# Transposing w_sg by DMA instead of on TensorE in a fused attention and gMLP kernel, with its step list ordered anew

## Chip, cores, metric

One core of one Trainium2 chip. The metric is the device time of one execution in microseconds (us). A run is called slow when it is more than 1.5% above the fastest run of the same kernel; in the rounds of the experiments the fast runs of the kernel before lie between 158.9 and 160.9 us. Ratios and verdicts use fast runs only; medians are over all runs.

## The reference

Windowed attention with four sink tokens, followed by a gMLP block. For each of 4 batches (8 heads, 768 positions, head size 64):

```python
scores = q @ k.T / sqrt(64)                # kept: the first 4 keys, and the last 128
x   = softmax(scores) @ v                  # heads side by side: 768 x 512
h   = gelu(x @ w_in)                       # 512 -> 1024; u = h[:, :512], v = h[:, 512:]
v_n = (v - mean) / sqrt(var + 1e-6) * g_ln
v_s = w_sg @ v_n + b_sg                    # w_sg is 768 x 768, over positions
out = x + (u * v_s) @ w_out
```

The kernel computes in bf16 with f32 accumulation. The spatial product needs `w_sg` with its rows turned into columns; `w_sg` is loaded once, turned once, and used by all four batches.

## The kernel before

The whole kernel is one list of steps. Every engine takes the instructions of its steps in the order of the list, so the list is the schedule. Nearly all loads are issued by GpSimd, also in list order, and stand among its other work. `mm_ring` is a ring of four PSUM buffers, `sc_ring` one of two: a step that takes a buffer waits until its last reader is done. In both kernels q and k of batch 3, and x of batches 2 and 3, are turned by DMA already.

| step | what it does | engine |
|---|---|---|
| `LQ LK LV LW LWS LWO` | loads of q, k, v, w_in, w_sg (two halves), w_out | GpSimd issues |
| `TQ`, `TK`; `EQ`, `EK` | turn four or two heads of q or k; copy from PSUM | TensorE; VectorE (`.D`) or ScalarE (`.A`) |
| `QK`, `EX`, `MK`, `SX` | scores, exponentials, masks, exponentials of the sinks | TensorE, ScalarE, VectorE or GpSimd, ScalarE |
| `AV`, `NR`, `XT`, `XE` | weighted values, normalisation, turn of x, its copy | TensorE, VectorE, TensorE, VectorE or ScalarE |
| `MA`/`MV`, `UA`/`MU`; `GV`, `GU` | w_in products, v half and u half; gelu | TensorE; ScalarE |
| `BN RS NM Z` | layer norm | VectorE, GpSimd, VectorE, both |
| `WT`; `WE` | turn a row block of w_sg; bring it into `wsgT` | TensorE; VectorE, or DMA |
| `SP`, `GT`, `GM` | spatial product, its bias, the gate | TensorE, VectorE, VectorE or GpSimd |
| `OU OB`, `RA RB`, `ST SB` | w_out product, addition of x, store | TensorE, VectorE, SyncE |

The first number of a step is the batch. The parts that matter here:

```python
def WT(ti):                                    # six turns on TensorE into one PSUM buffer
    fresh(mm_ring, ("w", ti))
    ps = psb(("w", ti))
    for si in range(NT):
        nc.tensor.transpose(ps[:, si, :], wsg_rows[:, ti, 128 * si:128 * (si + 1)], iden)

def WE(ti):
    if ("w", ti) not in mm_ring.held:          # no WT before it: one DMA transpose on SyncE
        return nc.sync.dma_start_transpose(out=wsgT[:, :, 128 * ti:128 * (ti + 1)], in_=wsg_rows[:, ti, :])
    nc.vector.tensor_copy(wsgT[:, :, 128 * ti:128 * (ti + 1)], psb(("w", ti)))

def SP(b, hf, dc):
    ps = fresh(mm_ring, ("g", b, hf, dc))
    for si in range(NT):
        nc.tensor.matmul(ps[:, 0:NH], z[b][:, si, 128 * dc:128 * (dc + 1)],
                         wsgT[:, si, NH * hf:NH * (hf + 1)], start=(si == 0), stop=(si == NT - 1))
# ... cut ...
for step in STEPS.split():
    name, *idx = step.split(".")
    done[step] = code[name](*(int(i) if i.isdigit() else i for i in idx))
```

The softmax here doesn't subtract the row's maximum and nothing guards it: scores larger than these inputs give would overflow.

Of the kernel before, what the change touches and what calls it, by code (L numbers as in the profile page):

```python
# [13 lines left out]


STEPS = """
ZERO IDEN LQ.0.0 LK.0.0 LQ.0.1 FILL LK.0.1 LC MASK VSK LK.0.2 MASK0 CQ.0.0.D LK.0.3 HM.7 TQ.0.0 CK.0.0.D LQ.0.2
EQ.0.0.A TK.0.0 LQ.0.3 EK.0.0.A TQ.0.1 LV.0.0 KS.0.0 QK.0.0.2 EQ.0.1.D QK.0.0.0 SK.0.0 EX.0.0.2 LV.0.1 VSM.0 TK.0.1
LV.0.2 EK.0.1.D HM.1 TK.0.2 EX.0.0.0 QK.0.0.1 LQ.1.0 MK.0.0.2.D KS.0.1 TK.0.3 EK.0.2.A LV.0.3 MK.0.0.0 QK.0.1.2 SK.0.1
EX.0.0.1 EK.0.3.D LW.0 SX.0.1 KS.0.2 QK.0.1.1 KS.0.3 LW.1 EX.0.1.2 MK.0.0.1.D TQ.0.2 TQ.0.3 EX.0.1.1 EQ.0.2.D QK.0.1.0  # L20
LWS.0 AV.0.0.1 EX.0.1.0 EQ.0.3.D QK.0.2.0 MK.0.1.1.P SK.0.2 EX.0.2.0 NR.0.0.1 AV.0.0.0 QK.0.3.1 LWS.1 NR.0.0.0 SK.0.3
EX.0.3.1 QK.0.3.0 MK.0.1.0 LQ.1.2 EX.0.3.0 QK.0.2.1 MK.0.1.2.D LK.1.0 AV.0.1.0 MK.0.2.0 AV.0.1.1 EX.0.2.1 MK.0.3.1.P
NR.0.1.0 QK.0.3.2 SX.0.3 QK.0.2.2 NR.0.1.1 EX.0.3.2 LK.1.2 TQ.1.0 MK.0.2.1.D XT.0.2 EX.0.2.2 LWO TQ.1.1 MK.0.3.0
EQ.1.0.A AV.0.2.0 XE.0.2.D MK.0.3.2.P EQ.1.1.A NR.0.2.0 AV.0.3.0 XT.0.0 MK.0.2.2.P NR.0.3.0 AV.0.3.1 XE.0.0.D LQ.2.0
XT.0.1 AV.0.2.1 NR.0.3.1 MA.0.0 XE.0.1.D NR.0.2.1 MV.0.0 VSM.1 LV.1.0 XT.0.3 GV.0.0 VSM.3 UA.0.0 VSM.2 MU.0.0 LG WT.1
LV.1.1 XE.0.3.A BN.0.0 WT.2 WT.0 GU.0.0 MV.0.2 WE.2 WE.1 MV.0.1 WE.0 LV.1.2 GV.0.2 BN.0.2 MU.0.3 GV.0.1 WT.3 BN.0.1
RS.0.2 GU.0.3 WT.5 TQ.1.3 LV.1.3 TQ.1.2 EQ.1.3.A MU.0.1 WE.5 RS.0.1 EQ.1.2.A WE.3 NM.0.2 MU.0.2 GU.0.1 LQ.2.2 Z.0.4.D
NM.0.1 Z.0.5.A Z.0.1.D TK.1.0 Z.0.3.D GU.0.2 TK.1.1 LV.2.0 Z.0.2.D TK.1.2 EK.1.0.A Z.0.0.D TK.1.3 EK.1.1.D EK.1.2.A
QK.1.0.2 QK.1.0.0 SP.0.0.2 EK.1.3.A EX.1.0.0 LV.2.1 KS.1.0 WT.4 SP.0.0.0 GT.0.0.2 WE.4 SK.1.0 GT.0.0.0 SP.0.1.2
EX.1.0.2 LV.2.2 MK.1.0.0 SX.1.0 GM.0.0.0.D QK.1.1.2 GT.0.1.2 QK.1.0.1 LK.2.0 TQ.2.0 EX.1.1.2 GM.0.0.2.D TQ.2.1  # L30
GM.0.1.2.D EX.1.0.1 SP.0.1.0 MK.1.1.2.D LK.2.2 MK.1.0.2.D EQ.2.1.A QK.1.1.0 MK.1.0.1.D QK.1.1.1 EQ.2.0.A SP.0.1.1
LV.2.3 GT.0.1.0 EX.1.1.1 AV.1.0.0 GM.0.1.0.P GT.0.1.1 AV.1.0.1 EX.1.1.0 NR.1.0.0 SP.0.0.3 GM.0.1.1.P NR.1.0.1 QK.1.2.2
LV.3.0 GT.0.0.3 QK.1.3.0 EX.1.2.2 SP.0.0.1 MK.1.1.1.D LV.3.1 EX.1.3.0 MK.1.1.0 TQ.2.2 AV.1.1.1 GT.0.0.1 MK.1.2.2.P
EQ.2.2.A QK.1.2.1 NR.1.1.1 QK.1.2.0 LV.3.2 EX.1.2.1 TQ.2.3 GM.0.0.1.D AV.1.1.0 GM.0.0.3.D EX.1.2.0 XT.1.2 LV.3.3
MK.1.3.0 OU.0.0 NR.1.1.0 EQ.2.3.A MK.1.2.1.P QK.1.3.1 XE.1.2.D QK.1.3.2 EX.1.3.1 XT.1.0 RA.0.0 OU.0.1 MK.1.2.0
EX.1.3.2 ST.0.0 LK.3.0 TK.2.0 XE.1.0.D AV.1.2.0 RA.0.1 EK.2.0.A AV.1.2.1 NR.1.2.0 ST.0.1 TK.2.1 MK.1.3.1.P TK.2.3
NR.1.2.1 EK.2.1.A TK.2.2 QK.2.0.0 EK.2.3.A EK.2.2.D MK.1.3.2.P QK.2.0.2 AV.1.3.0 EX.2.0.0 SP.0.1.3 NR.1.3.0 LK.3.2
EX.2.0.2 KS.2.0 AV.1.3.1 QK.2.1.2 GT.0.1.3 QK.2.1.1 EX.2.1.2 SK.2.0 NR.1.3.1 XT.1.1 MK.2.0.2.P EX.2.1.1 OU.0.2
XE.1.1.D GM.0.1.3.P SX.2.0 QK.2.1.0 RA.0.2 QK.2.0.1 EX.2.1.0 XT.1.3 LQ.3.0 MK.2.1.1.D OU.0.3 ST.0.2 XE.1.3.A
MK.2.1.2.D MV.1.0 MK.2.0.0 EX.2.0.1 RA.0.3 LQ.3.2 MK.2.0.1.D ST.0.3 MV.1.1 GV.1.0 MK.2.1.0 AV.2.1.0 OU.0.4 GV.1.1  # L40
BN.1.0 MV.1.2 EK.3.1 RA.0.4 MU.1.0 BN.1.1 GV.1.2 AV.2.0.1 ST.0.4 EK.3.2 GU.1.0 MU.1.3 BN.1.2 RS.1.1 OU.0.5 GU.1.3
NM.1.1 RS.1.2 MU.1.1 Z.1.3.A EK.3.3 RA.0.5 Z.1.0.A Z.1.1.D NM.1.2 MU.1.2 Z.1.2.A NR.2.1.0 Z.1.4.D GU.1.1 AV.2.0.0
Z.1.5.D EQ.3.0 GU.1.2 AV.2.1.1 NR.2.0.1 QK.2.2.0 NR.2.0.0 QK.2.2.2 SP.1.1.0 EX.2.2.0 NR.2.1.1 SP.1.0.0 ST.0.5 EQ.3.1
GT.1.1.0 GM.1.1.0.P SP.1.0.3 EX.2.2.2 GT.1.0.0 MK.2.2.0 QK.2.3.0 EQ.3.3 QK.2.2.1 GT.1.0.3 GM.1.0.0.P EX.2.3.0 SP.1.0.2
MK.2.2.2.D EX.2.2.1 SP.1.1.2 GM.1.0.3.D MK.2.3.0 EQ.3.2 QK.2.3.1 GT.1.1.2 MK.2.2.1.P QK.2.3.2 SP.1.1.1 EX.2.3.1
GT.1.0.2 GM.1.1.2.D EX.2.3.2 AV.2.2.0 MK.2.3.1.P EK.3.0 GT.1.1.1 SP.1.0.1 NR.2.2.0 GM.1.0.2.P AV.2.3.0 GT.1.0.1
QK.3.1.1 MK.2.3.2.P QK.3.1.2 NR.2.3.0 AV.2.2.1 EX.3.1.1 SP.1.1.3 XD.2.0 GM.1.0.1.P NR.2.2.1 EX.3.1.2 AV.2.3.1
MK.3.1.1.P GT.1.1.3 QK.3.0.1 NR.2.3.1 QK.3.0.0 MK.3.1.2.P EX.3.0.1 OU.1.1 EX.3.0.0 KS.3.0 OU.1.0 MK.3.0.1.P RA.1.1
XD.2.1 SK.3.0 RA.1.0 QK.3.0.2 SX.3.0 QK.3.1.0 OU.1.2 MK.3.0.0 EX.3.0.2 GM.1.1.1.D EX.3.1.0 AV.3.0.0 GM.1.1.3.D MV.2.0
MK.3.0.2.P RA.1.2 MK.3.1.0 ST.1.1 ST.1.0 ST.1.2 OU.1.3 GV.2.0 OU.1.4 MV.2.1 BN.2.0 MV.2.2 GV.2.1 RA.1.4 RA.1.3 ST.1.4  # L50
OU.1.5 GV.2.2 BN.2.1 ST.1.3 MU.2.2 BN.2.2 MU.2.0 RS.2.1 GU.2.2 MU.2.3 GU.2.0 NM.2.1 RS.2.2 RA.1.5 Z.2.3.A Z.2.0.D
ST.1.5 MU.2.1 Z.2.1.A NM.2.2 NR.3.0.0 GU.2.3 Z.2.5.D AV.3.1.0 Z.2.4.D GU.2.1 AV.3.0.1 NR.3.1.0 QK.3.3.1 QK.3.2.0
AV.3.1.1 EX.3.3.1 Z.2.2.D NR.3.0.1 SP.2.1.2 NR.3.1.1 SP.2.0.3 GT.2.1.2 EX.3.2.0 MK.3.3.1.P QK.3.3.0 GT.2.0.3 SP.2.1.3
EX.3.3.0 GM.2.1.2.D GM.2.0.3.D QK.3.2.1 MK.3.2.0 QK.3.3.2 SP.2.0.2 EX.3.2.1 MK.3.3.0 GT.2.1.3 EX.3.3.2 AV.3.3.0
MK.3.2.1.P GT.2.0.2 SP.2.0.1 NR.3.3.0 MK.3.3.2.P AV.3.2.0 GT.2.0.1 QK.3.2.2 SP.2.0.0 GM.2.0.2.P NR.3.2.0 EX.3.2.2
GM.2.1.3.D XD.3.0 AV.3.3.1 MK.3.2.2.P GT.2.0.0 SP.2.1.0 NR.3.3.1 GM.2.0.0.P AV.3.2.1 GT.2.1.0 SP.2.1.1 GM.2.0.1.D
NR.3.2.1 GM.2.1.0.P OU.2.0 GT.2.1.1 XD.3.1 OU.2.1 GM.2.1.1.D RA.2.0 OU.2.5 RA.2.1 MU.3.0 RA.2.5 MV.3.0 GU.3.0 ST.2.5
ST.2.0 ST.2.1 OU.2.2 GV.3.0 MV.3.1 BN.3.0 MV.3.2 GV.3.1 RA.2.2 BN.3.1 ST.2.2 MU.3.1 GV.3.2 OU.2.3 BN.3.2 RS.3.1 GU.3.1
MU.3.3 NM.3.1 RS.3.2 RA.2.3 Z.3.3.A MU.3.2 Z.3.2.D ST.2.3 Z.3.1.A NM.3.2 Z.3.0.D OU.2.4 Z.3.5.A Z.3.4.D GU.3.2
SP.3.0.1 RA.2.4 GU.3.3 ST.2.4 SP.3.0.2 GT.3.0.1 GM.3.0.1.P SP.3.0.3 GT.3.0.2 GM.3.0.2.D SP.3.0.0 GT.3.0.3 GM.3.0.3.P  # L60
SP.3.1.0 GT.3.0.0 GM.3.0.0.P SP.3.1.3 GT.3.1.0 GM.3.1.0.P OU.3.1 GT.3.1.3 SP.3.1.1 GM.3.1.3.P RA.3.1 ST.3.1 OU.3.0
GT.3.1.1 SP.3.1.2 GM.3.1.1.P RA.3.0 ST.3.0 OU.3.2 GT.3.1.2 GM.3.1.2.P RA.3.2 ST.3.2 OU.3.5 OU.3.3 RA.3.5 ST.3.5 OB.3.5
RA.3.3 OU.3.4 RB.3.5 ST.3.3 SB.3.5 RA.3.4 ST.3.4
"""


# [5 lines left out]
TURN = ('SSSS', 'SSSS', 'SSSS', 'DDDD')  # L72


LAST = (5,)


@with_exitstack
def kernel(
# [477 lines left out]
    def cols_of(b, t, second=False):  # L557
        n = d_model // 2 if b == B - 1 and t in LAST else d_model
        return slice(n, 2 * n) if second else slice(0, n)
# [74 lines left out]
```

## Time and profile before

| | us |
|---|---|
| two runs before the prediction | 161.38 and 159.85, median 160.62 |
| the profiled run of them (slow state) | 162.22 |
| the same kernel in the rounds of the experiments, medians | 159.25 to 159.71 |

The profiled run was in the slow state, and that mattered. Its page shows a lower granted clock in two early slices (third and fourth digit) and these transfers. The clock digits are tenths of full speed in 40 slices of the span, and q1 is the queue of the transfers that SyncE issues:

```profile
PEclk9968999999999999999999999999999999999998
...
DMA packets 63154, 22.70 MB, mean 141 GB/s; under 512 B 51360, under 2 KB 60064, under 8 KB 63136
...
q1 hardware_dynamic: 17648, 10.66, 25.6%
```

TensorE's stretches as the slow profile has them stand in the prediction below. There the first w_in product of batch 0 starts at 28.3 us and TensorE has hardly a gap after it (0.3 us up to 150 us). In the traced fast run of the old order (e3 below) that product starts at 24.4 us, and TensorE then comes to loads that have not landed, as the experiments show.

### The profile page before, as it was taken

What the parts mean: (1) busy time and instruction counts of PE and PEld (TensorE: products, weight loads), DVE (VectorE), ACT (ScalarE), POOL (GpSimd) and SP (SyncE); (2) the same over time, 40 slices, a digit from 0 to 9 for tenths busy, and PEclk for the clock granted to TensorE, in tenths of its full rate; (3) what the DMA queues carried; (4) which work ended last, traced back from release to release, by engine and by line L of the source; (5) the groups of instructions that cost most, each with busy time, mean ns of one, the idle gap of its engine ahead of it and who ended that gap; (6) DMA issues with size and microseconds to landing.
All of it is one profiled execution on the core that took longest, in us unless ns stands there. A gap on an engine that the chain in (4) does not pass through costs nothing.

```text
span 160.5 us, 3811 instructions
## 1 busy us (share of the span) xinstructions
PE 147.8 (92%) x1520; PEld 86.9 (54%) x1520; DVE 130.2 (81%) x303; ACT 99.9 (62%) x117; POOL 86.4 (54%) x118
## 2 busy tenths in 40 slices
PE   4588867999999999999999999999999999999980
PEld 1245456657656667655665673445756644555530
DVE  4459999979998999897798889689889945976661
ACT  3168995438999797995697747835986225480000
POOL 7996898226854999990405595204038600216620
PEclk9968999999999999999999999999999999999998
DMA  5999999999999999999997028430100592121144
GB/s 160 168 176 162 189 206 211 204 247 204 168 167 161 195 161 163 199 169 187 187 230 153 0 44 166 185 122 8 65 4 0 102 190 104 65 78 55 69 165 163
DMA packets 63154, 22.70 MB, mean 141 GB/s; under 512 B 51360, under 2 KB 60064, under 8 KB 63136
## 3 DMA queue, kind: packets, MB, share of 16 engines
q0 software_dynamic: 45488, 11.80, 80.1%
q1 hardware_dynamic: 17648, 10.66, 25.6%
q8 instruction: 12, 0.20, 0.5%
q14 instruction: 6, 0.05, 0.1%
HBM read 24.81 MB, written 6.29 MB: 194 GB/s over the span
## 4 chain that ended last, share of the span: by engine, by line
PE 76%; DVE 13%; DMA 4%; ACT 3%; issue 1%; POOLq 1%; POOL 1%; SPq 0%; DVEq 0%
PE mm L538 20%; PE mm L554 12%; PE sc L453 12%; PE sc L505 11%; PE sc L367 6%; PE mm L308 4%; PE mm L407 4%; DMA vt<-in_k_dram 4%; DVE P L382 3%; PE mm L413 2%; DVE z L496 2%; PE mm L417 2%; PE mm L436 2%; DVE x_sb L427 2%; DVE st L476 2%
## 5 line engine op out<-in xcount | busy, mean ns | idle before, releaser
L375 ACT ACTIVATE P<-sc 128x1024 bf16<-128x1024 f32 (+1 forms) x48 | 43.3, 967 | 8.0 <-PE sc L367 7.9
L538 PE MATMUL mm<-wsgT,z 128*128 128x384 bf16 x192 | 35.1, 326 | 0.1
L554 PE MATMUL mm<-w_out_sb,wsg_gated 128*128 128x512 bf16 (+1 forms) x100 | 23.7, 371 | 0.7 <-POOL wsg_gated L548 0.7
L538 PEld LDWEIGHTS <-z 128*128 128x128 bf16 x192 | 17.5, 98 | 12.3 <-issue 1.7
L548 POOL TENSOR_TENSOR wsg_gated<-gtmp,uT 128x384 bf16<-128x384 bf16 x17 | 15.9, 938 | 15.0 <-DVE gtmp L543 7.1
L543 DVE SCALAR_TENSOR_TENSOR gtmp<-mm,g_sb,b_bc 128x384 bf16<-128x384 f32 x32 | 19.6, 615 | 5.4 <-PE mm L538 4.6
L484 POOL TENSOR_TENSOR rs<-rs,neg_half 128x2 f32<-128x2 f32 (+1 forms) x8 | 6.9, 864 | 31.1 <-DVE rs L479 28.7
L505 PE MATMUL sc<-xT,w_in_sb 128*128 128x384 bf16 x128 | 22.4, 326 | 0.0
L476 DVE BATCH_NORM_STATS2 st<-vt 128x6 f32<-128x512 f32 x24 | 16.2, 675 | 7.4 <-ACT vt L467 7.4
L453 PE MATMUL sc<-w_in_sb,xT 128*128 128x512 bf16 x96 | 22.0, 379 | 0.0
L467 ACT ACTIVATE vt<-sc 128x1024 f32<-128x1024 f32 x12 | 12.2, 1024 | 14.7 <-PE sc L453 13.0
L386 POOL TENSOR_SCALAR_AFFINE_SELECT P<-P 128x512 bf16<-128x512 bf16 x20 | 13.0, 652 | 13.9 <-ACT P L375 13.8
L382 DVE TENSOR_TENSOR P<-P,mask 128x1024 bf16<-128x1024 bf16 (+1 forms) x28 | 20.0, 744 | 0.1
L562 DVE TENSOR_TENSOR ot<-mm,x_sb 128x512 f32<-128x512 f32 (+1 forms) x25 | 16.3, 663 | 3.7 <-PE mm L554 3.7
L221 POOL DMA_DIRECT2D v_sb<-in_v_dram x16 | 16.4, 1033 | 4.9 <-DMA wsg_gated<-in_moe_w_sg_dram 3.7
L427 DVE TENSOR_TENSOR x_sb<-mm,rcp 128x384 bf16<-128x384 f32 x32 | 17.8, 557 | 1.1
L521 ACT ACTIVATE uT<-sc 128x768 bf16<-128x768 f32 x16 | 12.6, 804 | 9.6 <-PE sc L505 9.6
L407 PE MATMUL mm<-v_sb,P 128*128 128x65 bf16 x192 | 16.6, 194 | 0.7 <-DVE P L382 0.7
L505 PEld LDWEIGHTS <-w_in_sb 128*128 128x128 bf16 x128 | 12.4, 98 | 8.7
L367 PE MATMUL sc<-qT,kT 64*128 64x256 bf16 x192 | 15.2, 267 | 1.9 <-ACT P L375 1.1
L407 PEld LDWEIGHTS <-P 128*128 128x128 bf16 x192 | 14.6, 98 | 4.2 <-DVE P L382 1.5
L413 PE MATMUL mm<-v_sb,P 128*128 128x65 bf16 x160 | 15.5, 194 | 0.0
(77 smaller groups left out, 222.3 us busy)
## 6 DMA issues: line engine op xcount, KB each, us to landing
out_dram<-ot SPq DMA_DIRECT2D x23, 256.0 KB, 2.8
v_sb<-in_v_dram POOLq DMA_DIRECT2D x16, 192.0 KB, 10.6
q<-in_q_dram POOLq DMA_DIRECT2D x4, 384.0 KB, 13.0
k<-in_k_dram POOLq DMA_DIRECT2D x4, 384.0 KB, 14.4
wsg_gated<-in_moe_w_sg_dram POOLq DMA_DIRECT2D x2, 576.0 KB, 14.3
w_in_sb<-in_moe_w_in_dram POOLq DMA_DIRECT2D x2, 512.0 KB, 12.0
kn<-in_k_dram POOLq DMA_DIRECT2D x4, 192.0 KB, 7.7
qn<-in_q_dram POOLq DMA_DIRECT2D x4, 192.0 KB, 6.9
```

The costliest lines, as they stand in the source:

```text
L367: nc.tensor.matmul(sc[:, hl, 256 * jl:256 * jl + n], kT[b, p][rows, 128 * j:128 * (j + 1)], qT[b, p][rows, 128 * j:128 * j + n], start=Tru ...
L375: nc.scalar.activation(out=pt[:, :, 0:w], in_=sc_ring[b, p, g][:, :, 0:w], func=AF.Exp, scale=scale)
L382: nc.vector.tensor_mul(pt[:, :, 0:w], pt[:, :, 0:w], m.unsqueeze(1).to_broadcast([128, 2, w]))
L407: nc.tensor.matmul(av[:, il, hl, :], P[b, p, i // 2][:, hl, 256 * (i % 2):256 * (i % 2) + 128], vb[:, h, i, :], start=first, stop=False)
L413: nc.tensor.matmul(av[:, il, hl, :], P[b, p, j // 2][:, hl, 256 * (j % 2) + 128:256 * (j % 2) + 256], vb[:, h, j, :], start=False, stop=False)
L427: nc.vector.tensor_mul(xs[:, 3 * half:3 * half + 3, :].rearrange("p t (h d) -> p t h d", h=H)[:, :, heads(b, p), :], av[:, :, :, 0:Dh], rc ...
L453: nc.tensor.matmul(hp[:, jl, :], xT[b][:, j, c, :], w_in_sb[:, c, d_half:2 * d_half], start=(c == 0), stop=(c == KD - 1))
L476: nc.vector.bn_stats(out=st, in_=vt[b, jj][:, jl, :])
L505: nc.tensor.matmul(hp[:, n, 0:NH], w_in_sb[:, c, 128 * dc:128 * (dc + 1)], xT[b][:, 3 * hf:3 * hf + 3, c, :], start=(c == 0), stop=(c == K ...
L538: nc.tensor.matmul(ps[:, 0:NH], z[b][:, si, 128 * dc:128 * (dc + 1)], wsgT[:, si, NH * hf:NH * (hf + 1)], start=(si == 0), stop=(si == NT ...
L543: nc.vector.scalar_tensor_tensor(out=gtmp.new((b, hf, dc)), in0=mm_ring["g", b, hf, dc][:, 0:NH], scalar=g_sb[:, dc:dc + 1], in1=b_bc[:, N ...
L554: nc.tensor.matmul(mm_ring["o", b, t][:, cols], gatedT[:, (2 * b + hf) % 3, dc, 128 * tl:128 * (tl + 1)], w_out_sb[:, dc, cols], start=(dc ...
```

## The change

The intent is to take 36 turns off TensorE and six copies off VectorE by letting six DMA transposes fill `wsgT`. The steps `WT.0` to `WT.5` are gone, so each `WE` becomes a DMA transpose. The last three output tiles are stored in halves (`OB`, `RB`, `SB` for tiles 3 and 4 too). The whole list is ordered anew, and some steps go to another engine with it: of the copies of turned q and k 14 stand on VectorE in place of 7. The core of the list, with most lines cut:

```diff
-KS.0.0 QK.0.0.2 EQ.0.1.D QK.0.0.0 SK.0.0 EX.0.0.2 LV.0.1 VSM.0 TK.0.1
+HM.2 QK.0.0.1 KS.0.0 LWO QK.0.0.2 SK.0.0 EX.0.0.1 VSM.0 TK.0.1 LV.0.1      # w_out's load early
 ... cut ...
-UA.0.0 VSM.2 MU.0.0 LG WT.1 ... MV.0.2 ... MV.0.1 ... MU.0.3 ... WT.3 ... WT.5 TQ.1.3 LV.1.3 TQ.1.2
+UA.0.0 GV.0.2 TQ.1.2 MU.0.0 LV.2.0 EQ.1.2.A BN.0.2 MU.0.3                  # a q turn ahead of u products
 ... cut ...
-QK.1.0.2 QK.1.0.0 SP.0.0.2 EK.1.3.A EX.1.0.0 ... WT.4 SP.0.0.0 ... SP.0.1.2 EX.1.0.2
+QK.1.2.2 EQ.1.3.D TK.1.1 EX.1.2.2 TK.1.3 QK.1.2.1 ... EX.1.2.1 QK.1.1.1 ... EX.1.1.1 QK.1.0.1 ... WE.5
+SK.1.0 EX.1.0.1 QK.1.0.0 ... QK.1.1.0 EX.1.0.0 SP.0.0.2                    # spatial products behind the scores
 ... cut ...
-LAST = (5,)
+LAST = (3, 4, 5)
```

## The prediction

> **What bounds the kernel now.** I read the page first, for the busy shares and the digits in 40 slices:
>
> ```profile
> span 160.5 us, 3811 instructions
> ...
> PE 147.8 (92%) x1520; PEld 86.9 (54%) x1520; DVE 130.2 (81%) x303; ACT 99.9 (62%) x117; POOL 86.4 (54%) x118
> ...
> PE   4588867999999999999999999999999999999980
> ...
> DMA  5999999999999999999997028430100592121144
> ```
>
> TensorE is full from the eighth slice to the last but one; DMA is full up to about 84 us. Then I cut the span into five stretches, in the view of busy time by window:
>
> ```profile
> 10.00:28.40 18.40, 15.07 (x254) 10.09 (x253) 17.30 (x34) 14.57 (x18) 15.29 (x21) 0.92 1.56 190
> 28.40:150.50 122.10, 121.80 (x1190) 71.52 (x1188) 103.61 (x244) 82.23 (x96) 60.24 (x77) 1.00 1.05 131
> 150.50:156.70 6.20, 5.44 (x30) 2.66 (x28) 4.10 (x8) 0.00 (x0) 1.82 (x2) 1.00 0.40 149
> 156.70:160.50 3.80, 0.00 (x0) 0.00 (x0) 0.66 (x1) 0.00 (x0) 0.00 (x0) 0.89 0.47 173
> ```
>
> The columns after the length are the busy us of TensorE, weight loads, VectorE, ScalarE and GpSimd. From 28.4 to 150.5 us TensorE is busy 121.80 of 122.10 us: whatever leaves its stream there comes off the end, if what follows is ready. In 10 to 28.4 us it is VectorE that is nearly full (17.30 of 18.40): the first batch's masks, copies and normalisations. After 156.7 us only one addition and a store remain. Last, the chain of waits in order of time, around what the change removes and at the end:
>
> ```profile
> 28.42 1.73 PE sc L453 x8
> 30.14 0.34 PE mm L436 x6
> 30.48 1.30 PE sc L505 x8
> 31.78 1.00 PE mm L528 x18
> ...
> 156.66 0.69 DVE ot L562
> ```
>
> The start of line 453 at 28.42 us is the first w_in product: everything before it is the head. Line 528 holds the turns of w_sg, 18 of them in 1.00 us on the path.
>
> **What the Trainium skill says.** "VectorE: DVE Perf Modes", section "The three transpose paths", has 390 ns for TensorE and 1309 ns for DMA, for one 128x128 bf16 block, and says that TensorE ends in PSUM and DMA in SBUF. The trace differs on what matters here: a turn lasts 219 ns and pipelined turns follow each other every 56 ns (1.00/18), and a DMA transpose of six blocks takes 1.2 to 1.46 us of SyncE's queue. So per block neither figure of the page is the cost. "DMA: Bandwidth & Descriptors", section "SWDGE vs HWDGE vs iDMA", says that transposes issued from SyncE and loads issued from GpSimd sit in different internal queues of the same 16 engines, between which each engine goes round robin. The trace agrees that they share: the qn load that was landing while two transposes ran took 2.85 us after its predecessor (77.12 to 79.97), the ones ahead of it 1.7 and 1.6 us. "Perfetto Trace Analysis", section "Identifying the Most-Contended Engine", warns that matmul busy time is no measure of closeness to the peak and names weight-load share instead: here 71.52 of 122.10 us, 59%. I therefore use busy time only to find that TensorE has no gaps, and take the cost of a turn from the pace of the chain, not from its duration.
>
> **The change part by part.**
>
> (1) The six steps WT go. Each is 6 turns, so 36 turns at 56 ns: 2.0 us off TensorE, all between 31 and 46 us, inside the stretch where it has no gaps. With them go six copies from PSUM (groups by line: busy us, mean ns of one, idle before):
>
> ```profile
> L528 PE MATMUL mm<-iden,wsg_gated 128*128 128x128 bf16 x36 | 2.5, 219 | 0.0
> L533 DVE COPY wsgT<-mm 128x768 bf16<-128x768 bf16 x6 | 3.0, 544 | 0.0
> ```
>
> The copies are 3.0 us of VectorE and six turns of the four-buffer PSUM ring. VectorE is not the bound after 28.4 us (103.6 of 122.1), and the new steps fill what is freed: copies of turned k and q on VectorE go from 7 to 14 (7 x 0.95 us), the masks from 12 to 13 (those with a letter), against 3 fewer of x (0.55) and 6 fewer gate products (0.37). Adding all these durations up, VectorE's total stays within 1 us. ScalarE loses about 3 us, GpSimd gains about 4; neither is near its limit. None of this moves the end by itself.
>
> (2) Six DMA transposes are added, each of a w_sg row block into wsgT. The same form exists for batch 3 (issues of the page, median us to landing):
>
> ```profile
> kT<-kn SPq DMA_TRANSPOSE x4, 4.6
> qT<-qn SPq DMA_TRANSPOSE x4, 4.4
> ```
>
> That is 4.4 to 4.6 us from issue to landing (5.0 at worst, while loads still ran), 1.4 us apart on the queue. Three can start when the first half of w_sg has landed, three after the second. How late that is, I work out from the order of loads. One after another the loads land at the intervals measured before: w_sg half 2.83 us, w_out 2.54, w_in halves 2.15 and 2.54. The new order puts w_out and the first w_sg half ahead of w_in. So v's last pair lands at about 21.2 + 2.5 = 23.7, w_sg's first half at 26.5, w_in's first half at 28.7 (23.3 before), its second at 31.2, and the second w_sg half, after q and k of batch 1, near 42. The masks of GpSimd stood between loads before and left a hole of some 1 us (k landed at 8.12, then 10.26), which the new order partly closes; so all this may be up to 1 us earlier. The first three transposes land near 31.5, 33 and 35; the last three near 47 to 51. Their readers: the first spatial product waits for three blocks and now stands behind six groups of scores and the four k turns of batch 1, near 45; the second half's products stand some 10 us later still, near 55. Both have slack of several us. So the 4.5 us of a transpose should be hidden, and with it the 2.0 us are really gone.
>
> (3) Their price is bandwidth. From the qn pair above, two transposes cost the load queue 2.85 - 1.6 = 1.25 us, about 0.65 each. Three of them fall between w_sg's first half and k of batch 1, which without them would land near 38.98 + 2.54 - 2.84 = 38.7 (w_out moved ahead, second w_sg half moved behind). With three it is 40.6, or 39.6 if the hole closes. TensorE turned the first k of batch 1 at 41.64 us. Before that step its new stream has 3.4 us less by the durations of the groups (five WT of 0.33 are gone; one product of u, 1.30, and one turn of q, 0.46, lie later now), so it wants k at about 38.3. A gap of 0 to 2.5 us may open there; I take 1.2.
>
> (4) The head. My sums of VectorE's durations before the first w_in product are 22.9 us for the new order and 21.8 for the old, with GpSimd 22.9 against 22.1, and w_in now lands at 28.7 or a little less where 28.4 is the old start. The new order is free to overlap better (q's cast on ScalarE, scores that need no sink first, two extra warming products). I take +0.3 us, with 1.5 either way.
>
> (5) The end. The last tile's addition was 0.69 us for 512 columns; the 256-column form in the same trace takes 0.42. A store of 128 KB landed in 1.70 us, one of 256 KB in 2.00. Halving the three last tiles therefore takes 0.27 + 0.30 = 0.57 us off the end. TensorE's columns stay the same (24 products of 256 in place of 8 of 256 and 8 of 512); the eight more additions, loads of weights and stores lie beside it, at 0.43 us per half against 0.42 per addition, 0.34 per store issue.
>
> Sum: -2.0 + 1.2 + 0.3 - 0.6 = -1.1 us, which gives 159.5 from the median of 160.6. As the steps were ordered anew as a whole, around the freed engine time, I trust my two penalties less than the two gains and halve them: -1.9, so 158.7 us.
>
> **The rivals.** (a) The turns were hidden, and the path merely moves: nothing comes off, 160 to 161 us, as TensorE then waits for z or for k. For it: the chain of waits from 34.5 to 44 us runs through batch norm and z on ScalarE and VectorE, not through TensorE; against it: TensorE is still 5.70 us busy of the 6 from 40 to 46. (b) The wait for a turn becomes a wait for a transfer: DMA is full until 84 us, the transposes or the k and w_in loads behind them arrive late, and TensorE stands 3 to 4 us near 29 or 38 us; time 161 to 163. For it: the landing sums above, close to the needs; against it: the new order puts the spatial products far back, as if the transfers' times were known. (c) The reorder is better than my sums say: the head, where TensorE does some 20.5 of 28.4 us, shrinks by 1.5 to 2 us more, with the full 2.0 and 0.6: 156 to 157. For it: room is there; against it: VectorE is full there and gets no lighter, and w_in comes later.
>
> **Range and chances.** 158.7 us, with 156.7 to 160.7 as the eight-in-ten range: its lower end is (c), its upper end (a). Faster by over 2% needs about 157.4 or less (160.6 x 0.98), thus both gains whole and a head shorter by a further us: 0.2. Slower by over 2% needs rival (b) at its worst: 0.05. Within 2%: 0.75.
>
> **What would show it.** Right: no instructions of the turns and copies of w_sg, six transposes of 4.4 to 6 us landing; TensorE without gaps from the first w_in product to 150 us, that stretch about 2 us shorter; the last addition near 0.42 us, and 3.2 us instead of 3.8 from the end of TensorE to the end of the span. Step 3 right: a gap of about 1 us ahead of k's turn of batch 1, released by the k load. Wrong: waits on wsgT by the spatial products; a first w_in product later than 30 us (b) or before 27.5 (c); or a stretch of TensorE that isn't shorter.

## The result

The changed kernel takes 168.64 us (two fast runs, 168.41 and 168.87). The ratio to the kernel before is 1.0542, with a 95% interval of 1.0405 to 1.068. Ratios here are the mean time of one kernel's fast runs over that of the other's of the same rounds, so not quite the ratio of the quoted medians. The change is 5% slower; 158.7 us and a chance of 0.05 for slower by over 2% had been predicted.

The page of the changed kernel, in the lines that answer to those before:

```profile
span 167.2 us, 3756 instructions
...
PE   4876649999789698999999999999999999999980
...
PEclk9999975899969999999999999999999999999999
DMA  5999999999999999999999936811100445111064
...
DMA packets 68242, 23.86 MB, mean 143 GB/s; under 512 B 56193, under 2 KB 65409, under 8 KB 68225
...
q1 hardware_dynamic: 22736, 11.84, 30.8%
```

TensorE's digits show holes up to the 16th slice, two half-clock stretches appear (digits 7, 5 and 8, then 6), and q1 has 5,088 packets more. Of those 288 come with the halved stores (runs with the new tail and no transposes on w_sg have 17,936), so a transpose of 192 KB is 800 packets: in the trace's packet records 768 of 256 bytes and 32 of 4 bytes.

The view of busy time by window of the changed kernel (columns as in the prediction; the granted clock is the third from the end):

```profile
24.40:31.00 6.60, 6.58 (x94) 5.75 (x91) 4.37 (x11) 1.64 (x3) 3.67 (x5) 0.57 1.25 203
...
40.00:50.00 10.00, 8.21 (x122) 4.92 (x120) 7.83 (x17) 9.97 (x13) 5.24 (x7) 0.86 1.61 163
50.00:70.00 20.00, 17.96 (x241) 11.54 (x238) 16.57 (x31) 10.02 (x13) 14.59 (x19) 0.99 2.36 158
```

Beside it the old order in a fast run (the kernel before with its last three tiles in halves, a run described below that takes the same time as before):

```profile
24.40:31.00 6.60, 6.21 (x54) 3.62 (x51) 6.36 (x17) 2.44 (x3) 2.09 (x3) 1.00 1.19 208
...
40.00:50.00 10.00, 9.79 (x118) 6.08 (x119) 8.45 (x22) 9.88 (x13) 5.71 (x7) 1.00 2.25 166
50.00:70.00 20.00, 20.00 (x276) 12.26 (x274) 17.63 (x40) 17.70 (x21) 18.97 (x24) 1.00 2.14 183
```

From 40 to 70 us TensorE stands 3.8 us in the changed kernel (1.79 + 2.04) and 0.2 us in the old order. Nearly everything is lost before batch 1 (9.1 us of the 9.8 between the spans): the first w_in product of a batch, read from the trace, starts at these times in us, and from batch 1 to batch 3 all kernels take 61 to 62 us.

| kernel | batch 0 | batch 1 | batch 3 | end of TensorE | span |
|---|---|---|---|---|---|
| before, slow profile | 28.3 | 69.8 | 130.9 | 156.6 | 160.5 |
| old order, fast (e3) | 24.4 | 66.5 | 127.7 | 153.6 | 157.3 |
| changed | 30.8 | 75.6 | 137.5 | 163.4 | 167.2 |

What TensorE waited for up to 75 us in the changed kernel (us in total, times, longest):

```profile
PE sc L367 <- ACT P L375: 3.6, 6, 1.3
PE mm L308 <- ACT exs L358: 3.0, 2, 1.9
...
PE mm L407 <- DMA v_sb<-in_v_dram: 2.0, 2, 1.1
```

Scores wait for exponentials, turns of q and k for a PSUM buffer that the sink exponentials hold, weighted values for the load of v. No spatial product waits for `wsgT`: the new order puts its readers far enough back. But the transposes are slow (duration of the issue in ns as minimum, median, maximum; then us from issue to landing, which the trace gives for two of the six):

```profile
L532 SPq DMA_TRANSPOSE wsgT<-wsg_gated x6: 1212/2031/8591, 25.6 to 45.8; - x6
...
DMA to landing us min/median/max: 9.5/10.9/12.3
```

The end of the chain of waits shows the tail in halves:

```profile
160.99 0.44 DVE ot L562
...
161.47 1.92 PE mm L554 x16
...
163.41 0.42 DVE ot L562
163.84 0.33 DVEq L629
```

The last addition takes 0.42 us as predicted, but from the end of TensorE's work to the end of the span it is still 3.8 us (163.4 to 167.2).

### The profile page after: what moved, and what is told of

It reads as the page before. It is cut to its first block, busy times and chain, and to the rows that moved or that the text cites. A ratio compares the mean times of both kernels' runs of the same rounds, so it can differ in the third digit from the quotient of the medians.

```text
span 167.2 us, 3756 instructions
## 1 busy us (share of the span) xinstructions
PE 148.7 (89%) x1480; PEld 88.6 (53%) x1494; DVE 131.0 (78%) x298; ACT 98.1 (59%) x113; POOL 91.1 (55%) x122
## 3 DMA queue, kind: packets, MB, share of 16 engines
q1 hardware_dynamic: 22736, 11.84, 30.8%
## 4 chain that ended last, share of the span: by engine, by line
PE 57%; DMA 22%; POOL 8%; issue 6%; DVE 4%; POOLq 1%; DVEq 0%
DMA v_sb<-in_v_dram 14%; PE mm L538 12%; PE mm L554 10%; PE sc L505 9%; PE sc L453 9%; DMA w_in_sb<-in_moe_w_in_dram 9%; PE sc L367 4%; POOL wsg_gated L548 4%; PE mm L308 3%; PE mm L407 2%; POOL v_sb L221 2%; PE mm L184 2%; PE mm L413 2%; PE mm L417 1%; POOL q L195 1%
## 5 line engine op out<-in xcount | busy, mean ns | idle before, releaser
L375 ACT ACTIVATE P<-sc 128x1024 bf16<-128x1024 f32 (+1 forms) x48 | 43.8, 958 | 15.9 <-PE sc L367 14.4
L538 PE MATMUL mm<-wsgT,z 128*128 128x384 bf16 x192 | 34.4, 327 | 0.0
L548 POOL TENSOR_TENSOR wsg_gated<-gtmp,uT 128x384 bf16<-128x384 bf16 x23 | 22.2, 969 | 14.0 <-DVE gtmp L543 13.4
L538 PEld LDWEIGHTS <-z 128*128 128x128 bf16 x192 | 17.5, 98 | 13.2 <-issue 2.7
L554 PE MATMUL mm<-w_out_sb,wsg_gated 128*128 128x512 bf16 (+1 forms) x100 | 22.6, 354 | 1.0 <-POOL wsg_gated L548 0.6
L382 DVE TENSOR_TENSOR P<-P,mask 128x1024 bf16<-128x1024 bf16 (+1 forms) x29 | 21.1, 737 | 1.2 <-ACT P L375 0.8
L367 PE MATMUL sc<-qT,kT 64*128 64x256 bf16 x192 | 16.5, 271 | 4.6 <-ACT P L375 3.6
L407 PE MATMUL mm<-v_sb,P 128*128 128x65 bf16 x192 | 18.2, 200 | 2.4 <-DMA v_sb<-in_v_dram 2.0
L484 POOL TENSOR_TENSOR rs<-rs,neg_half 128x4 f32<-128x4 f32 (+1 forms) x8 | 6.9, 866 | 23.2 <-DVE rs L479 21.5
L467 ACT ACTIVATE vt<-sc 128x1024 f32<-128x1024 f32 x12 | 12.3, 1024 | 10.8 <-PE sc L453 9.3
L407 PEld LDWEIGHTS <-P 128*128 128x128 bf16 x192 | 15.7, 102 | 5.1 <-issue 1.2
L386 POOL TENSOR_SCALAR_AFFINE_SELECT P<-P 128x512 bf16<-128x512 bf16 x19 | 12.2, 641 | 10.8 <-ACT P L375 10.8
L413 PE MATMUL mm<-v_sb,P 128*128 128x65 bf16 x160 | 17.1, 199 | 0.0
L505 PEld LDWEIGHTS <-w_in_sb 128*128 128x128 bf16 x128 | 12.3, 98 | 8.6
```

What stands on the lines that cost most here:

```text
L367: nc.tensor.matmul(sc[:, hl, 256 * jl:256 * jl + n], kT[b, p][rows, 128 * j:128 * (j + 1)], qT[b, p][rows, 128 * j:128 * j + n], start=Tru ...
L375: nc.scalar.activation(out=pt[:, :, 0:w], in_=sc_ring[b, p, g][:, :, 0:w], func=AF.Exp, scale=scale)
L382: nc.vector.tensor_mul(pt[:, :, 0:w], pt[:, :, 0:w], m.unsqueeze(1).to_broadcast([128, 2, w]))
L407: nc.tensor.matmul(av[:, il, hl, :], P[b, p, i // 2][:, hl, 256 * (i % 2):256 * (i % 2) + 128], vb[:, h, i, :], start=first, stop=False)
L413: nc.tensor.matmul(av[:, il, hl, :], P[b, p, j // 2][:, hl, 256 * (j % 2) + 128:256 * (j % 2) + 256], vb[:, h, j, :], start=False, stop=False)
L505: nc.tensor.matmul(hp[:, n, 0:NH], w_in_sb[:, c, 128 * dc:128 * (dc + 1)], xT[b][:, 3 * hf:3 * hf + 3, c, :], start=(c == 0), stop=(c == K ...
```

## The experiments

Eighteen kernels ran. Their expectations speak of two theories: T, the transposes' traffic beside the loads makes the changed kernel slow; O, the new order does. Old and new order mean the lists of before and after. "Free" means that nothing turns w_sg and the spatial products read columns of w_in in its place: the same instructions and shapes, a wrong result on purpose.

| run | order before / after the first w_in product | w_sg turned by | us (median) | ratio to before | first w_in product, batch 0 / 1 |
|---|---|---|---|---|---|
| e3 | old / old, new tail | TensorE | 159.68 | 0.9991 | 24.4 / 66.5 |
| e6 | old / old | free | 159.37 | 0.998 | 25.2 / 66.6 |
| e1 | old / old | DMA | 173.6 | 1.0772 | 25.8 / 82.2 (slow) |
| e5 | new / new | free | 166.17 | 1.0407 | 30.0 / 73.0 |
| e2 | new / new | TensorE | 170.14 | 1.0562 | 33.5 / 79.7 (slow) |
| e18 | old / new | free | 166.5 | 1.0455 | 25.3 / 73.4 |
| e19 | old / new | TensorE | 167.74 | 1.0532 | 24.7 / 75.2 |
| e9 | old / new | DMA | 171.76 | one look | 25.4 / 77.6 |
| e10 | new / old | TensorE | 165.71 | 1.0374 | 30.2 / 73.1 |

The medians of e1, e2 and e9 have slow runs in them, and the traced runs of e1 and e2 are slow ones. Their fast runs took 171.9 and 172.4 us (e1), 168.5 and 169.1 (e2), 169.7 and 170.8 (e9). The record's verdict is "unclear" for e1, e2, e4 and e13, although the intervals of their ratios all lie above 1.03; for e9 it has no ratio.

### The three parts of the change, one at a time

**e3: the old order with the halved tail.**

```diff
-LAST = (5,)
+LAST = (3, 4, 5)
-... OU.3.5 OU.3.3 RA.3.5 ST.3.5 OB.3.5 RA.3.3 OU.3.4 RB.3.5 ST.3.3 SB.3.5 RA.3.4 ST.3.4
+... OU.3.4 OU.3.5 RA.3.4 OB.3.4 RA.3.5 ST.3.4 OB.3.5 RB.3.4 ST.3.5 OU.3.3 RB.3.5 SB.3.4 OB.3.3 SB.3.5 RA.3.3 ST.3.3 RB.3.3 SB.3.3
```

> The kernel before with the last three tiles in halves, nothing else. Both theories: 0.4 to 0.7 us faster than before (addition 0.42 in place of 0.69 us, store of 128 KB in place of 256 KB).

159.68 against 159.62 us, ratio 0.9991 (0.997 to 1.0013): nothing, where both theories had 0.4 us or more. Its chain ends like this:

```profile
153.65 0.42 DVE ot L562
154.07 0.33 DVEq L629
```

The last addition ends at 154.41 us by the records, against 154.23 in the old order free of turns (e6). The last store is issued at 154.56 against 154.26, because three short stores stand one behind the other on SyncE (0.37, 0.55 and 0.36 us each). The 0.27 us saved in the addition goes into more additions and issues.

**e6: the old order, free.**

```diff
-WT.0 ... WT.5 WE.0 ... WE.5
-                         wsgT[:, si, NH * hf:NH * (hf + 1)],
+                         w_in_sb[:, si % KD, NH * hf:NH * (hf + 1)],
```

> Wrong result on purpose: the old order with neither turns nor transposes, products as in the run before this one. Both theories: what the six turns and copies are worth where nothing replaces them, 2.0 us off before: 157.3 to 158. If the turns were hidden: 159.3 to 160.

159.37 against 159.71 us, ratio 0.998 (0.9959 to 1.0001). All 36 turns and six copies are gone, about 2 us of TensorE, and the end moves by less than 0.4%. What fills the place shows in what TensorE waited for from 31 to 50 us:

```profile
PE mm L307 <- DMA q<-in_q_dram: 0.9, 1, 0.9
```

TensorE comes earlier to the turns of batch 1's q and waits for its load, which lands at 34.4 us. In e3, with the turns of w_sg ahead of it, the same turn of q starts at 34.9 us without a wait. So the turns stood in a hole that the load leaves. (The traces show only 0.9 of the 2 us there; in this run of e6 the head also came 0.8 us later to the first w_in product than in e3.) This is rival (a) of the prediction, with q's load in place of k or z as what TensorE waits for.

**e1: the old order with the six transposes in place.**

```diff
-WT.1 WT.2 WT.0 WT.3 WT.5 WT.4
```

> The order and the tail of the kernel before; the six turns of w_sg and their copies are taken out and the six DMA transposes put in their places. Theory T (the transposes' packets share the DMA engines with the saturated load queue: each transpose is slow to land, 9 to 12 us, and takes 1.6 us or more from the loads): spatial products wait for w_sg, time 163 to 167. Theory O (the new order of steps is what is slow, the transposes are nearly free): 158 to 161.

Fast runs of 171.9 and 172.4 us, ratio 1.0772 (1.0648 to 1.0896): slower than either theory had it. TensorE waits for the transposes themselves (its waits from 24 to 75 us, in a slow run):

```profile
PE mm L538 <- DMA wsgT<-wsg_gated: 10.7, 2, 7.5
```

The two transposes whose landing the trace gives took 13.2 and 14.5 us.

**e4: the kernel before with six transposes that nobody reads**, three after w_in has landed and three after a load of q.

```diff
+    dead = sb.tile([128, NT, S], BF16, name="dead")
+    def WX(ti):
+        return nc.sync.dma_start_transpose(out=dead[:, :, 128 * ti:128 * (ti + 1)], in_=w_in_sb[:, 0, 0:S])
-HOLDS = "LG<LWS.0"
+HOLDS = "LG<LWS.0 WX.1<LW.1 WX.5<LQ.2.0"
-MU.0.0 LG WT.1
+MU.0.0 WX.1 WX.2 LG WX.0 WX.5 WX.4 WX.3 WT.1
```

> The kernel before with six dead DMA transposes of the same form and size (a column block of w_in into a tile that nobody reads), three released by the load of w_in, three by the load of q of batch 2. Nothing waits for them except the SyncE queue behind. Theory T: the loads of batch 1 and 2 land 3 to 9 us later, the dead transposes need 8 to 12 us, and the time grows by what batch 1's v and k are late, 1 to 4 us. Theory O: time within 0.5 us of before.

171.69 us, ratio 1.0722 (1.0625 to 1.082); theory T had 1 to 4 us. No other engine waits for a dead transpose, so these 12 us are the price of the transposes' presence beside the loads. TensorE's waits in the same stretch:

```profile
PE mm L308 <- DMA q<-in_q_dram: 6.8, 1, 6.8
PE mm L308 <- DMA k<-in_k_dram: 1.5, 1, 1.5
```

The load that it waits for longest, the last pairs of batch 2's q, lands at 62.6 us, 12.7 later than in e3 (49.9).

**e11: the same six dead transposes near 107 to 115 us**, when the loads are done.

```diff
-BN.2.1 ST.1.3
+BN.2.1 WX.0 WX.1 WX.2 WX.3 WX.4 WX.5 ST.1.3
```

> The kernel before with the same six dead DMA transposes as in the slow dead run, but issued after the stores of batch 1, near 105 us, where the load queue is done. If it is the loads beside them that make transposes dear: each lands in 3.5 to 5 us, time within 0.5 us of before (12 us more where they met the loads). If transposes are dear by themselves or hold SyncE's stores up: 2 us or more above before.

159.65 against 159.64 us, ratio 0.9997 (0.9971 to 1.0024). The view of the tile `dead` (the traced run is a slow one, with its half clock long before, at 24.8 to 28.3 us):

```profile
L538 SPq DMA_TRANSPOSE dead<-w_in_sb x6: 1262/1286/1290, 107.7 to 114.3; - x6
...
DMA to landing us min/median/max: 2.8/2.8/2.8
```

Alone a transpose lands in 2.8 us; beside the loads, the same instruction took 10.3 and 13.4 us (e4, the two landings that its trace gives). The packet records show why. A packet of a transpose lasts 18 ns here and 31 ns beside loads; there, about as many records of loads stand beside those of transposes (264 and 257 from 36 to 38 us of e4), and they last 78 to 135 ns each. If each of the 50 packets on each of 16 engines waits for one packet of a load, a transpose takes 4 to 7 us, an estimate from these records without what the queue adds. In the records the packets of the first transpose of e4 take 5.6 us to move, in place of 1.1 in e11.

**e5: the new order, free** (from the kernel after, as e6 from before).

```diff
-WE.0 ... WE.5
+                         w_in_sb[:, si % KD, NH * hf:NH * (hf + 1)],
```

> Wrong result on purpose: the new order and tail, with neither turns nor transposes of w_sg; the spatial products read columns of w_in instead, of the same shape. It shows what the order itself costs. Theory O (order: w_in 5 us later, waits of TensorE on the sink exponentials, throttled clock after them): 164 to 168. Theory T (the transposes' traffic alone makes the changed kernel slow): 156 to 159.

166.17 us, ratio 1.0407 (1.0367 to 1.0447). So the new order costs 6.5 us by itself, with no turn and no transpose of w_sg at all; the transposes add 168.64 - 166.17 = 2.5 us to it. These two kernels did not run in the same rounds; e8 below, the changed kernel with one step moved, did run beside e5, and its ratio of 1.0569 says the same. The landing times of the loads in the traces, changed kernel against e5, give the transposes' price for the load queue: k of batch 1 lands at 40.1 against 37.7 us when the packets of two transposes have moved (1,536 of 256 bytes; 1.2 us each), the last pair of v of batch 1 at 57.3 against 48.5 when those of all six have (8.8 us, 1.5 each). The v load that TensorE waits for near 55 us in the changed kernel is one of those delayed.

**e2: the new order with the turns put back**, each `WT` right ahead of its `WE`.

```diff
+WT.1 WE.1 ... WT.2 WE.2 ... WT.0 WE.0 ... WT.5 WE.5 ... WT.4 WE.4 ... WT.3 WE.3
```

> The new order and tail, but w_sg turned on TensorE with VectorE copies at the same places. Theory T: the loads of batch 1 come on time again, only the 2.4 us of the head stay lost: 162 to 164, despite 2.0 us more TensorE work. Theory O: 168 to 171, as slow as the changed kernel or slower by the turns.

170.14 us with slow runs among them (168.49 to 172.84), verdict unclear. It does not test what it should: a turn with its copy right behind it makes VectorE, which takes its steps in order too, wait for TensorE (3.6 us in three waits up to 75 us, in a slow run). Its failure led to e5.

### Where the new order loses: the head?

In the changed kernel the first w_in product comes at 30.8 us, 6.4 later than in a fast run of the old order, about as much as the new order costs in e5. The theory formed from that was that the head, which is all work ahead of that product, loses the time. Four causes were visible there: w_out and half of w_sg are loaded ahead of w_in, which lands at 28.1 us in place of 23; the sink exponentials of the last heads stand behind all others on ScalarE; VectorE has all normalisations behind a copy of q; and TensorE's clock is halved from 23.3 to 30.1 us. All but VectorE's order were undone in turn, in the changed kernel or in e10.

**e7 (loads), e8 (sink exponentials), e12 (both).**

```diff
 e7:  -LWO between KS.0.0 and QK.0.0.2      +LWO behind LK.1.2
      -LWS.0 behind EX.0.1.1                +LWS.0 behind LW.1
 e8:  -MK.0.3.0 SX.0.3 MK.0.2.0             +QK.0.3.1 SX.0.3 EX.0.3.1
 e12: both
```

> The changed kernel with two loads moved: w_out behind k of batch 1, the first half of w_sg behind w_in. w_in then lands near 23 us in place of 28. If the load order is what makes the head slow: first w_in product near 26 to 28 us in place of 30.8 and 2 to 4 us off the time. If the head is slow for another reason (TensorE's wait for the sink exponentials): the product stays near 30 us, time within 1 us of the changed kernel.

> The changed kernel with one step moved: the exponential of the sinks of heads 2 and 3 before the last two exponentials of batch 0, so that the PSUM buffer that the first turn of batch 1 needs is free 2 us earlier. If TensorE's wait there, and the throttled clock from 24 to 31 us after it, make the head slow: the clock stays near full, first w_in product near 28.3 us (then held by w_in's load), 2 to 3 us off. If not: within 0.5 us of the changed kernel.

> The changed kernel with both single moves at once: w_out and w_sg behind w_in, and the sink exponential earlier. Each alone gained nothing. If the two held each other (w_in at 28.1 us, PSUM buffer at 24): first w_in product near 27 us. If a third thing holds the head (masks and normalisations on VectorE, the throttled clock): near 30 us again. The time also carries that w_sg and q, k of batch 1 now land close together with the transposes, as in the run with the loads alone moved, so 167 to 171 either way.

170.82, 168.86 and 169.38 us, ratios 1.0679, 1.0569 and 1.0607. None is faster than the changed kernel; e7, meant to be within 1 us of it, is 2 us slower. In e7 w_in has landed at 23.2 us, and its product still starts at 30.7; in e12 at 30.4.

**e10: the new head with the old rest; e13: the same with 23 dummy products.** A dummy multiplies the identity into a PSUM buffer that is written afresh later, to keep TensorE busy.

```diff
 e10: new steps up to MA.0.0, then the old steps with turns and old tail
 e13: +HW.1.2 ... +HW.1.2 ... +HW.1.5 ... +HW.0.3 ... +HW.1.2 ... +HW.1.1 ... +HW.1.8
```

> The other way round: new order up to the first w_in product, then the old order with TensorE turns and the old tail. If the head is the whole cost of the order: product near 30 us, 164.5 to 167. If the rest of the new order is slow: 160 to 162.

> The kernel of new head and old rest (165.7 us) with 23 dummy products of 512 columns put into TensorE's waits of the head (12 to 15 us, and 18 to 24 us), written to PSUM buffers that are free at that moment. If the half clock that follows poorly filled windows (15.6 to 19.0 and 25.9 to 29.3 us in the trace without them) is what makes the head slow: no half clock in the trace, first w_in product at 28.2 us or a little before 29 (w_in lands at 28.1), 2 to 4 us off: 162 to 163.7. If the clock is only a symptom, the waits themselves being what costs: the same 165.5 to 166.

165.71 and 165.18 us, ratios 1.0374 and 1.0355, in different rounds. The dummies lift the profile's mean clock from 0.975 to 0.998 and gain at most 0.5 us. So the half clock is mostly a sign of the waiting, not its cause. e10 is no clean test of the head, because the second half of w_sg, which the new head loads late, lands at 40.7 us, and the old rest turns it early: TensorE waits 1.2 us for it.

**e14 (the changed kernel with dummies), e15 (the same with w_out late), e17 (the kernel before with seven dummies).**

```diff
 e14: +HW at the seven places of e13, +HW.0.5 and +HW.0.2 among batch 1's exponentials
 e15: e14, -LWO behind KS.0.0, +LWO behind LK.1.2
 e17: +HM.2 +HM.3 +HW.1.2
```

> The changed kernel with the same dummy products, and seven more ahead of two groups of scores of batch 1, where TensorE waits for ScalarE near 45 us. Clock theory: no half clock, 3 to 5 us off the changed kernel: 163.5 to 165.5; what is left over before is w_in 5 us late and the transposes. Otherwise 168 to 169.

> As the run before, with w_out loaded behind k of batch 1 as well, so that v of batch 0 and w_in land 2.5 us earlier. If w_in's load is the next thing that holds the head: first w_in product near 26 us and 2 us more off: 161.5 to 163.5. If the late q, k and v of batch 1 hold the middle anyway: no better than the run before.

> A try at beating both: the kernel before with seven dummy products in three waits of its head (before the first k turn, the second q turn, one group of scores of head 3). The kernel before loses about 3 us in those of its runs in which a half-clock window falls into its head (161.5 to 162.4 against 159.3). Clock theory: fewer such runs, fast runs the same, median 159 to 159.6. If the dummies stand in the way: 160 to 161.

169.42, 168.91 and 159.81 us; ratios 1.0614, 1.0581 and 1.0034. At a clock of 0.998 to 1.0, and with the first product at 29.0 us (e15), the changed kernel gains nothing; nor does the old order gain from dummies.

**e9: the old head with the new rest and transposes.**

```diff
 old steps up to MA.0.0, then the new steps, all six WE as transposes, new tail
```

> Old order up to the first w_in product (batch 0's attention and its loads), new order, DMA transposes and tail from there on. By the run of the new order without any turns, the order alone costs 6.5 us and is complete by the first w_in product (30.0 us in place of 24.4). If the head is the whole cost of the order: the product starts near 25 us, and of the 9 us only the transposes' part stays: 161 to 164. If the rest is slow too: 166 to 169. In this version both halves of w_sg are loaded ahead of batch 1's q and k, so six transposes may meet those loads; a k that is late can hide part of the gain.

Fast runs of 169.7 and 170.8 us, and two slow ones: the first product is at 25.4 us, 5.4 earlier than in the changed kernel (168.64), and still no run is shorter. Both expectations, 161 to 164 and 166 to 169 us, were too low. Either the transposes fall on a worse place, or the head is not the cause.

### Or the order after it?

**e18: e9 free; e19: e9 with the turns on TensorE, each some steps ahead of its copy.**

```diff
 e18: -WE.0 ... WE.5, the spatial products read w_in_sb
 e19: +WT.1 WT.2 WT.0 behind MU.0.0, +WE.1 WE.2 WE.0 behind BN.0.2
      TQ.2.1 +WT.5 EQ.2.0.D +WE.5 ... SP.0.0.2 +WT.4 ... GT.0.0.2 +WE.4 ... SP.0.0.3 +WT.3 ... GT.0.0.3 +WE.3
```

> Steps of before up to the first w_in product, then the steps of the changed kernel, without turns and without transposes (the spatial products read columns of w_in, so the result is wrong on purpose). Theory (the new order costs time only in its head, by the first w_in product; the rest of it costs nothing of its own): first w_in product at 24 to 26 us, 159 to 160.5 us, within 1% of the kernel before. Rival (the order after the head costs by itself too): first product as early, but 162 us or more.

> The same steps as the run beside it, but with the six TensorE turns and their VectorE copies put back, each a few steps ahead of its first reader; the result is right. Theory (head and transposes are the whole cost of the change): 159 to 161 us, within 1% of the kernel before and of the run beside it, since the turns are hidden. Rival (the order after the head costs, or leaves the turns no hidden place): 162.5 us or more.

166.5 us (1.041 to 1.05) and 167.74 us (1.0458 to 1.0607). The head as the only cause falls. e18 has the old head, an early first product (25.3 us), no turns and no transposes, and it is as slow as e5, which has the product at 30.0 us: batch 1 starts at 73.4 and 73.0 us. The 5 us that the new head is late are not what sets the new order's time, which is why no repair of the head helped.

Where e18 loses them, in busy time by window, first the old order free (e6):

```profile
31.00:40.00 9.00, 7.86 (x110) 4.96 (x108) 7.58 (x20) 7.15 (x10) 5.94 (x6) 1.00 1.33 223
40.00:50.00 10.00, 9.59 (x114) 5.60 (x110) 7.52 (x19) 9.43 (x12) 5.40 (x6) 1.00 2.26 168
```

then e18:

```profile
31.00:40.00 9.00, 5.85 (x63) 3.44 (x62) 3.75 (x12) 3.83 (x5) 4.81 (x5) 1.00 1.33 223
40.00:50.00 10.00, 6.73 (x96) 3.98 (x93) 9.01 (x18) 9.72 (x13) 5.37 (x8) 0.86 3.23 150
```

and what TensorE waited for in e18 in the same 19 us:

```profile
PE mm L307 <- DMA q<-in_q_dram: 3.1, 1, 3.1
PE sc L366 <- ACT P L374: 2.4, 3, 1.7
```

TensorE is busy 4.9 us less (12.58 against 17.45), and runs at half clock from 47.3 to 50.7 us, worth up to 1.7 us more. Together that is 6.6 us, and batch 1 starts 6.8 us later (73.4 against 66.6). Two places of the list stand behind it:

- The first turn of batch 1's q behind the head, `TQ.1.2`, stands between the two halves of the first u product. TensorE comes to it at 31.9 us and stands until q has landed, at 35.0, with two and a half u products right behind that need nothing of it. In the old order one and a half more products lie ahead of its first turn of q there (in e6 it waits 0.9 us), and ScalarE, which needs the u products for its next work, is busy 7.15 us in place of 3.83 from 31 to 40.
- The spatial products of batch 0 stand behind the scores of batch 1. In the old order they start at 40.2 us (e6) and lie between those scores, so TensorE has work while ScalarE does the exponentials. In e18 they start at 50.0 us. From 41 to 50 us TensorE has only turns of q and k and scores, and the scores wait for exponentials to free one of two PSUM buffers (2.4 us in three waits). ScalarE is full there in both orders (9.43 and 9.72 of 10 us), but the first exponential, with the load of its table, begins at 43.55 in place of 41.04 us.

In e5 and in the changed kernel the head hides the first of the two: TensorE comes late, and q has landed. The second is the same in both (8.21 of 10 us busy from 40 to 50, the first spatial product at 49.9 us in e5). The line of e5:

```profile
40.00:50.00 10.00, 8.21 (x123) 4.82 (x122) 8.42 (x17) 9.97 (x13) 4.62 (x7) 0.83 2.91 157
```

That these two places are the cause is read from the trace; that the order behind the head costs 7 us is shown by e18. Moving the two groups back one at a time was not run, and no run separates the new order from the engines that some of its steps went to. The new head is not free either: in front of the old rest (e10) it costs some 6 us, less what its late w_sg half takes there. The two losses do not add up (6.5 us together in e5); that both end at the same chain of q, k and exponentials of batch 1 would explain it, but was not tested.

Whether the new rest hides the turns stays open: e19 is 1.2 us above e18 by the medians, and the intervals overlap.

No version beat the kernel before by more than 0.2% in ratio (e6, whose result is wrong).

## Why the prediction was wrong, step by step

- **The bound.** "whatever leaves its stream there comes off the end, if what follows is ready" was read from a profile in the slow state, where TensorE comes 4 us later to the first w_in product and finds everything ready. In a fast run what follows is not ready: q lands at 34.4 us, and e6 removes the work and gains nothing clear of noise. Step (1), -2.0 us, measured -0.3 (ratio 0.9959 to 1.0001).
- **Step (2), hidden transposes.** The readers did not wait, as said. But the first two transposes landed in 9.5 and 12.3 us, not 4.4 to 6: at 35.1 and 39.3 us where 31.5 and 33 were worked out. The 4.4 us came from a place where the loads were nearly over.
- **Step (3), bandwidth.** The mechanism was right: transposes delay the loads behind them. That k of batch 1 landed at 40.1 us, within the 39.6 to 40.6 predicted, is luck. Without transposes it lands at 37.7 (e5) and not at 38.7, and it was delayed by two transposes at 1.2 us each and not by three at 0.65. The gap ahead of its turn did not open either, since TensorE came there only at 40.8 us. The later transposes were left out of the sum, because their own readers had slack; the loads of v behind them had none. The net price in the new order is 2.5 us, against 1.2 taken and then halved. In the old order it is 12 us (e4).
- **Step (4), the head, +0.3 us, the one step that put a price on the new order. This is the step that failed.** Its working covered VectorE's durations and w_in's landing before the first product. w_in landed at 28.1 us, as worked out (28.7), and the product came at 30.8, 2.4 us later than in the slow profile and 6.4 later than in a fast run. The prediction's sign for rival (b), a first product later than 30 us, thus came true for another reason: with w_in there at 23.2 us (e7) the product still starts at 30.7. And its working stops there. The order behind the head was taken to be worth nothing, or even good ("ordered anew as a whole, around the freed engine time, I trust my two penalties less"). By itself, the new order costs 6.5 us (e5), and its rest costs 7 us behind the old head (e18). Sums of durations could not show it: VectorE's total, as step (1) has it, hardly changes, and TensorE and ScalarE got less work. What changed, as the trace of e18 reads, is which work stands beside the wait for q and beside the exponentials. Step (2) noted that the spatial products now stand behind the scores, counted it as slack for the transposes, and did not ask what would fill TensorE in their old place. That the order costs this is shown; which of its places do is read from one trace and was not tested.
- **Step (5), the end, -0.57 us**, measured 0 (e3): the addition did get shorter, but the last one ends no earlier and the stores queue.
- **The sum that the runs give:** 159.7 (before) + 6.5 (order) + 2.5 (transposes) = 168.7 us. It closes on the 168.64 measured by construction, since the 2.5 us are the rest that e5 leaves. Rival (a) was right that the turns were hidden. Rival (b) was right that the loads would be late: TensorE stood 2.0 us for v, though not where (b) had it; its 161 to 163 us were too little for want of the order.

## What to carry to other kernels

Before reading a bound from a profile, look at its state: work that is on the path in a slow run can lie in a hole in a fast one. When a list is ordered anew, check for every long wait on a load and every run of exponentials which independent work stood beside it, and whether it still does; sums of busy time cannot see this. A transfer off the path is not free while loads are queued: put dead copies of it into the old kernel and time them, once beside the loads and once in a quiet place.

## What the Trainium skill lacked or had wrong

- "Advanced Engine Details and Errata", section "X-Bar Transpose (TRN2)", says that "TRN2 transpose DMAs are as fast as regular DMAs". Here a transpose of 192 KB lands in 2.8 us in a quiet place (e11), where a plain store of 256 KB lands in 2.0 us (kernel before). The page does not tell what happens beside queued loads: 9.5 to 14.5 us to landing, and a delay of the loads, so that six transposes that nobody reads cost 12 us of 160 (e4).
- "VectorE: DVE Perf Modes", section "The three transpose paths", ranks the paths by time per block. Six blocks per DMA transpose came to 2.8 us (0.47 us a block) when quiet, and taking the turns off TensorE gained at most 0.3 us by the medians (e6); that section lacks that the cost depends on what else is in the queues.
- "TensorE: Matmul & The Clock Gate", section "Why this matters for your kernels", advises against gaps of TensorE over some 3 us to keep the clock. Half-clock stretches of 6.8 and 3.4 us came in the changed kernel after 3.4 us in which TensorE was busy for 1.49 and 1.61 us (44 and 47%), with no single wait over 2 us; the page's section "A second HAM failure mode: psum-queue depth-cycling" tells of a like case. It lacks that restoring the clock with dummy products need not restore time: 0.998 in place of 0.975 and 0.968, and a gain of at most 0.5 us (e13) or none (e14).
